# A two-layer mixture of experts on one core: the order of its head, and an eight-byte gather ahead of the first gather

## The chip, the cores and the metric

The kernel runs on one core of a Trainium2 chip. The metric is device time in microseconds (us) of one execution, and times are given as medians over runs. A profiled execution gives the span from the first to the last instruction; the execution's own time lies a little above it.

## The reference, cut to what matters

Three layers follow each other on 7168 tokens of 192 numbers: a causal convolution whose seven weights per token and head come from a softmax, and two mixtures of experts with eight experts each (two experts a token in the first, one in the second).

```python
def _attn_ref(x, weight_gen):
    w = weight_gen - np.max(weight_gen, axis=-1, keepdims=True)
    w = np.exp(w)
    w = w / (np.sum(w, axis=-1, keepdims=True) + 1e-09)
...
    out = np.einsum('bshk,bskhg->bshg', w, x_unf)

def _moe_ref(x, w_gate, w_noise, noise, w1, w2):
    logits = x @ w_gate
    noise_scale = np.log1p(np.exp(x @ w_noise))
    noisy_logits = logits + noise_scale * noise
    top2 = np.argpartition(-noisy_logits, 2, axis=1)[:, :2]
...
            h = np.maximum(x[mask] @ w1[e], 0.0)
            out[mask] += top2_w[mask, k, None] * (h @ w2[e])

def _moe2_ref(x, w_gate, w1, w2):
    expert_idx = np.argmax(logits, axis=1)
...
        h = np.maximum(xe @ w1[e], 0.0)
        ye = h @ w2[e]
        out[mask] = gate_w[mask, None] * ye
```

## The kernel before

The kernel writes all engines' instructions in one program, and a small scheduler decides their order while the program is built. Each piece of work is a generator (a thread of `Feed`, line 212) that yields the engine and the tiles it will need next. A `Clock` (line 78) keeps an estimate of when each engine and tile is free; `Feed.until` and `Feed.pump` always let the thread with the smallest estimated start go on, plus a bias in microseconds that was given when the thread was added (a negative bias favours it). Nothing of this runs on the chip: what is left is a fixed order on each engine's queue, and each queue is strictly in order. Nearly all instructions are recorded through one helper, so they carry line 190 in the profile and are told apart by their tiles.

The tokens of the first routed phase are 2 half batches of 12 token columns; the convolution treats them as six items of four columns: items 0 to 2 of the first half batch, 3 to 5 of the second. For an item VectorE multiplies tokens by softened weights, two taps at a time (`TAPS`, three steps of 1536 numbers a partition and one of 768, tile `prod`, three buffers: `PB`), and TensorE sums them with products by the identity (tile `acc`, two products of 128x384 a tap, each of which the profile counts as two records; 28 records an item). Then `split_rows` (622) scales the sum and splits it into two halves of fp16 (tiles `sx`, `rows`), the rows go to memory, are transposed (`xtg`), and `logit_thread` (707) multiplies them by the gate's weights (`gwh`, `gwl`, result `pm`, then `lg`).

Before that, `first_loads` (755) brings tokens and convolution weights, `first_soft` (794) softens the weights in four pieces (tile `wmxa`, a piece of 4 and one of 8 columns for each half batch; the weights themselves lie in `wres`), and `prep_gate` (428) loads the gate's weights (`gwr`), squares them on ScalarE (sum `gwa`), sums that over partitions with one product of the ones matrix on TensorE (into `pm`) and scales them on VectorE (`gwt`, `gwh`, `gwl`). `weight_lane` (469) does the same with the experts' weights in pieces W1 and W2 of 0.79 MB, two lanes of two buffers (`w`, sum `wacc`, product into `pm`, scale `wsc`); the first pieces are loaded by GpSimd's queue once a copy (`spacer`) has seen the first half batch's last tokens. After item 5, `choose` and `route_` (1048) pick the experts and compute the indices of the blocks (`sli`: block numbers, `src`: rows to gather), TensorE does 64 products without use (`NFILL`), and the experts begin: GpSimd gathers 128 rows at a time (`gt`), TensorE transposes the first ones (`ph` from `gt`), multiplies by W1 and W2 and so on to the end of the program.

Of the kernel before, what the change touches and what calls it, by code (L numbers as in the profile page):

```python
# [8 lines left out]
F32 = mybir.dt.float32  # L9
# [7 lines left out]
P = 128  # L17
D = 192
E = 8
# [10 lines left out]
W1FIRST = 0  # L30
CLATE = 20.0
W2LATE = -0.1
WLATE = 0.0
W1LATE = 0.0
PLATE = -2.0
VPE = -100.0
# [18 lines left out]
HT = 2  # L55
TP = 1
LT = 0.0
NFILL = 64
TB = 2
AB = 1  # L60
OBG = 0
# [211 lines left out]
def moe_kernel(ctx: ExitStack, tc: tile.TileContext, x: bass.AP, wgen: bass.AP,  # L273
               g1: bass.AP, n1: bass.AP, noise: bass.AP, w11: bass.AP, w12: bass.AP,
               g2: bass.AP, w21: bass.AP, w22: bass.AP, out: bass.AP):
    nc = tc.nc
# [3 lines left out]
    feed = Feed(clk)  # L280
    nc.scalar.preload_act_table_set("natural_log_exp_and_others")

    def new_pool(name, side=None, **kw):
        if side:
            kw["side"] = side
        return Pool(tc.alloc_tile_pool(name=name, bufs=1, **kw), clk, name.startswith("ps"))
# [19 lines left out]
    def small_ps():  # L306

        while ps_lock:
            yield None
        ps_lock.append(1)  # L310
        return psum.tile([P, 512], F32, name="pm")
# [12 lines left out]
    for pi, (m, g, ja, jb, full) in enumerate(((0, 0, 0, JS, True), (0, 0, JS, JA, False), (0, 1, JA, J, False),  # L324
                                               (1, 0, 0, JA, True), (1, 1, JA, J, False))):
        ph = Ph()
# [42 lines left out]
    raw = new_pool("raw", side="right")  # L369
# [55 lines left out]
    gw = [None, None]  # L425
    ngs = [2 * E, E]

    def prep_gate(m):
        srcs = [g1, n1] if m == 0 else [g2]
        n = E * len(srcs)  # L430
        a = raw.tile([P, 2, n], F32, name=f"gwr{m}")
        for i, s in enumerate(srcs):
            SP.dma_start(a[:, 0, i * E:(i + 1) * E], s[0:P])
            SP.dma_start(a[0:64, 1, i * E:(i + 1) * E], s[P:D])
            SP.dma_start(a[64:P, 1, i * E:(i + 1) * E], s[P:D])
        h = const.tile([P, 2, n], F16, name=f"gwh{m}")
        acc = const.tile([P, 1], F32, name=f"gwa{m}")
        yield "A", a
        A.activation(h, a, AF.Square, accum_out=acc)
        yield "P", acc  # L440
        ps = yield from small_ps()
        yield "P", acc, ps
        PE.matmul(ps[:, 0:1], onesf, acc, start=True, stop=True)
        t = const.tile([P, 4], F32, name=f"gwt{m}")
        yield "V", ps[:, 0:1]
        pow2(ps[:, 0:1], t[:, 0:1], t[:, 1:2], t[:, 2:3], 10)
        ps_lock.clear()
        lo = const.tile([P, n], F16, name=f"gwl{m}")
        V.tensor_scalar(h, a, t[:, 1:2], None, op0=ALU.mult)
        V.scalar_tensor_tensor(lo, a[:, 0], t[:, 1:2], h[:, 0], op0=ALU.mult, op1=ALU.subtract)  # L450
        V.scalar_tensor_tensor(h[64:P, 1], a[64:P, 1], t[64:P, 1:2], h[64:P, 1],
                               op0=ALU.mult, op1=ALU.subtract)
        gw[m] = (h, lo, t[:, 2:3])
# [301 lines left out]
    def first_loads():  # L755
        h = K - 1
        for b in range(B):
            G.memset(x0[b][0:1, 0:h], 0.0)
        def weights(b, a, z):
            SP.dma_start(g0[b][:, a * H:z * H].rearrange("p a k -> p (a k)"), bass.AP(  # L760
                tensor=wgen.tensor, offset=wgen.offset + (b * S + a) * H * K,
                ap=[[J * H * K, P], [1, (z - a) * H * K]]))

        def tokens(b, a, z):
            SP.dma_start(x0[b][:, h + a:h + z].rearrange("p j d -> p (j d)"), xrows(b, 0, P, a, z - a))

        for b in range(B):
            yield "S", x0[b]
            weights(b, 0, NJ)
            tokens(b, 0, NJ)  # L770
            for p0, np_ in ((16, P - 16), (1, 15)):
                SP.dma_start(x0[b][p0:p0 + np_, 0:h].rearrange("p j d -> p (j d)"), xrows(b, p0, np_, -h, h))
            tokens(b, NJ, 2 * NJ)
            weights(b, NJ, JS)
            tokens(b, 2 * NJ, JS)
            if b == 0:

                G.tensor_copy(spacer, x0[0][0:1, h + JS - 1, 0:1])
            loaded.append(b)
# [14 lines left out]
    def first_soft():  # L794
        for b in range(B):
            for a, z in ((0, NJ), (NJ, JS)):
                mx = raw.tile([P, JS * H], F32, name="wmxa")[:, 0:(z - a) * H]
                yield from soften(g0[b][:, a * H:z * H], mx, z - a)
                soft0[b].update(range(a, z))
                yield ()  # L800

    def conv_lane(items, early, pool, ln):
# [40 lines left out]
        while cur:  # L843
            r, i = cur
            lane_th[ln][2] = 0.0 if phases[1].ready else CLATE if r.g else BLATE if r.j0 and not started else 0.0
            b, ja, n = subs_of(r)[i]
# [29 lines left out]
            if on_pe:  # L876
                acc = psp.tile([P, 2, 512], F32, name=f"acc{ln}")
                k = 0
                for m in TAPS:
                    t = raw.tile([P, max(TAPS), NJ * D], F32, name="prod", bufs=PB)[:, 0:m, 0:n * D]  # L880
                    yield "V", t
                    taps(t, k, m)
                    yield "P", t, acc
                    for i in range(m):
                        for a in range(0, n, 2):
                            PE.matmul(acc[:, a // 2, 0:2 * D], identf, t[:, i, a * D:(a + 2) * D],
                                      start=(k + i == 0), stop=(k + i == K - 1))
                    k += m
                acc = acc[:, 0:n // 2, 0:2 * D].rearrange("p a (b d) -> p a b d", b=2)
                t = t[:, 0].rearrange("p (a b d) -> p a b d", b=2, d=D)  # L890
            else:
                acc = pool.tile([P, NJ, D], F32, name=f"acc{ln}", bufs=1 if ln else AB)[:, 0:n]
                prod(acc, 0)
                last = None
                for k in range(1, K):
                    yield "V",
                    t = pool.tile([P, NJ, D], F32, name="tmp", bufs=TB)[:, 0:n]
                    prod(t, k)
                    if k == K - 1 and q and XB == 1 and not ln:
                        nxt = yield from load(*q)  # L900
                    if last is not None:
                        V.tensor_tensor(acc, acc, last, op=ALU.add)
                    last = t
                yield "V",
                V.tensor_tensor(acc, acc, last, op=ALU.add)
# [142 lines left out]
    def route_(r):  # L1048
        ph, nt = r.ph, r.nt
# [145 lines left out]
        sf, si = [rt.tile([P, 2 * NTM], dt, name=v)[:, 0:nc2 * nt] for v, dt in (("slf", F32), ("sli", I32))]  # L1195
# [42 lines left out]
        for k, (reg, c0, n) in enumerate(groups):  # L1238
# [11 lines left out]
            for v in range(n):  # L1250
                PE.matmul(tp[:, reg * nb:(reg + 1) * nb], oh[:, :, v], ob[:, :, v],
                          start=(lo + v == 0), stop=(lo + v == 15 or c0 + v == nw - 1))
        if r is rts[0]:
            idle = psp.tile([P, 2, 512], F32, name="acc0")
            for _ in range(NFILL):
                nc.tensor.matmul(idle[:, 0, 0:P], ident, ident, start=True, stop=True)
# [156 lines left out]

    queue, lqueue, turned, pending, routing = [], [], [], [False] * 4, []
    todo = {"load": 0, "turn": 0}
    lane_th, w_th = [], []
    pools = []

    def hurry():
# [23 lines left out]
    gps = {(0, g): new_group(0, g) for g in range(2)}  # L1443
    rts = [new_route(ph, gps[0, ph.g]) for ph in phases[:3]]
    feed.add(first_loads(), -9.0)
    feed.add(first_soft(), -1.0)
    logit_ths = [feed.add(turn_thread(), LLATE), feed.add(logit_thread(), LLATE)]
    items = [(r, i) for r in rts for i in range(r.n)]
    early = [(r, i) for r, i in items if r is rts[0] or r is rts[1] and i < BPE]
# [3 lines left out]
    pieces = [(e, k) for e0 in range(0, E, WG) for k in range(2) for e in range(e0, e0 + WG)]  # L1453
    for k in range(2):
        w_th.append(feed.add(weight_lane(0, f"w{k}", pieces, k), WLATE))
    feed.add(prep_gate(0))
    feed.add(prep_gate(1))

    def noises():
        for r in rts:  # L1460
# [294 lines left out]
    for i in range(nu + 1):  # L1755
# [30 lines left out]
        n = max(n1, n2)  # L1786
# [66 lines left out]
```

## Time and profile before

| what | value |
|---|---|
| median of 3 runs (lowest to highest) | 982.63 us (980.37 to 986.98) |
| the profiled execution, its own time | 985.76 us |
| its span | 983.9 us |
| mean granted TensorE clock | 0.964 of 2.4 GHz |
| TensorE busy | 901.3 us (92%) |
| VectorE, ScalarE, GpSimd busy | 754.2, 514.0, 429.7 us |
| last convolution sum of the first phase ends | 88.64 us |
| first product of the experts begins | 129.63 us |

The profile is of one execution. A row of a timeline gives a start, a length and the instruction; in brackets stands how long its engine had been idle and what ended that. PE is TensorE, PEld its weight loads, DVE VectorE, ACT ScalarE, POOL GpSimd, SP the engine that issues most DMAs. The clock column is the clock granted to TensorE as a share of 2.4 GHz; 0.50 is 1.2 GHz.

### The profile page before, as it was taken

The page shows a single profiled execution, that of the slowest core. Times are in us where ns is not written, and L with a number is a line of the kernel's source. Part 1 is how long each engine was busy: PE and PEld are TensorE (multiplying, and loading weights), DVE is VectorE, ACT ScalarE, POOL GpSimd, SP SyncE. Part 2 cuts the span into 40 slices and gives each one's busy share as a digit, 9 for nine tenths or more (in the row PEclk, how much of TensorE's full clock was granted, in tenths as well). Part 3 has the DMA queues.
Part 4 walks back from the last instruction along what each step waited for, and adds up shares of the span by engine and source line. Part 5 has one row for each costly group of instructions (what it writes and reads, how often), then busy time and mean ns, then how long its engine had stood idle before and what let it go on. Part 6 is the DMA issues. An engine that isn't in the chain of part 4 may idle for free. (4 is left out here: it accounts for less than half of the span.)

```text
span 983.9 us, 26950 instructions
## 1 busy us (share of the span) xinstructions
PE 901.3 (92%) x10522; PEld 834.1 (85%) x10522; DVE 754.2 (77%) x1827; ACT 514.0 (52%) x1040; POOL 429.7 (44%) x574
## 2 busy tenths in 40 slices
PE   1897388899999999999999998999989999999996
PEld 0554388899998999999999998989989999999986
DVE  8587887889998999978498787798588886355453
ACT  1334068674533454653487797645766533444332
POOL 4020044565544555543454453343554544564552
PEclk8898599999999999999999999999999999999998
DMA  9256059968542895852478999853677447462692
GB/s 283 70 136 145 1 152 266 253 156 193 149 116 64 182 215 99 232 131 75 108 200 195 264 264 230 200 121 100 168 173 172 114 123 225 88 118 80 200 258 85
DMA packets 206161, 157.56 MB, mean 160 GB/s; under 512 B 134412, under 2 KB 184927, under 8 KB 206028
## 3 DMA queue, kind: packets, MB, share of 16 engines
q1 hardware_dynamic: 187292, 110.93, 46.2%
q0 software_dynamic: 18736, 44.85, 17.9%
q8 instruction: 84, 1.38, 0.6%
q14 instruction: 49, 0.40, 0.2%
HBM read 74.46 MB, written 32.59 MB: 109 GB/s over the span
## 5 line engine op out<-in xcount | busy, mean ns | idle before, releaser
L190 ACT ACTIVATE hh<-ph 128x512 f16<-128x512 f32 x362 | 214.8, 595 | 261.9 <-PE ph L190 254.8
L190 DVE SCALAR_TENSOR_TENSOR hl<-ph,hh 128x512 f16<-128x512 f32 x362 | 245.6, 684 | 108.7 <-ACT hh L190 100.5
L190 PE MATMUL ph<-xt,wres 128*128 128x256 f16 (+1 forms) x3200 | 320.9, 252 | 4.4 <-ACT xt L190 1.4
L190 PEld LDWEIGHTS <-wres 128*128 128x128 f16 x3200 | 261.5, 99 | 24.4 <-issue 3.9
L190 PE MATMUL py<-wres,hh 128*128 128x192 f16 x2048 | 273.1, 247 | 1.0 <-ACT yo L190 0.8
L190 PEld LDWEIGHTS <-hh 128*128 128x128 f16 x2896 | 260.6, 98 | 5.8 <-issue 1.7
L190 POOL DMA_INDIRECT gt<-rows,src x181 | 197.4, 1091 | 139.4 <-issue 119.7
L190 PE MATMUL py<-wres,hl 128*128 128x192 f16 x1024 | 252.5, 247 | 0.0
L190 POOL DMA_INDIRECT ybuf<-yo,dest x120 | 134.0, 1116 | 250.6 <-ACT yo L190 234.0
L190 PEld LDWEIGHTS <-hl 128*128 128x128 f16 x1448 | 141.9, 98 | 0.5 <-DVE hl L190 0.4
L190 PE MATMUL ph<-xt,w 128*128 128x128 f16 (+1 forms) x1600 | 135.4, 238 | 3.7 <-DMA w<-wres 2.0
L190 PEld LDWEIGHTS <-w 128*128 128x128 f16 x1600 | 113.9, 98 | 10.4 <-DVE w L190 2.6
L190 PE MATMUL py<-w,hh 128*128 128x192 f16 x848 | 113.2, 246 | 0.0
L190 POOL DMA_INDIRECT out_dram<-yo,dest x61 | 62.1, 1018 | 113.9 <-ACT yo L190 71.7
L190 PE MATMUL py<-w,hl 128*128 128x192 f16 x424 | 104.3, 246 | 0.2 <-DVE hl L190 0.2
L190 PE MATMUL acc<-prod,identf 128*128 128x384 f32 x168 | 62.1, 528 | 13.1 <-DVE prod L190 10.7
L190 PEld LDWEIGHTS acc<-prod,identf 128*128 128x128 f32 x168 | 33.8, 206 | 35.4 <-DVE prod L190 10.7
L190 DVE COPY w<-wres 128x3072 f16 x53 | 51.2, 967 | 8.2 <-issue 5.2
L190 DVE SCALAR_TENSOR_TENSOR wres<-w,wsc,wres 128x1024 f16<-128x1024 f32 (+1 forms) x32 | 49.6, 1550 | 7.6 <-ACT wres L190 6.9
L190 ACT ACTIVATE yo<-py 128x192 f32<-128x192 f32 x120 | 37.8, 328 | 28.2 <-PE py L190 22.8
L190 ACT ACTIVATE wres<-w,wsc 128x1024 f16<-128x1024 f32 (+1 forms) x32 | 43.5, 1361 | 10.1 <-DVE wsc L190 9.3
L190 ACT ACTIVATE wres<-w 128x1536 f16<-128x1536 f32 x32 | 47.3, 1477 | 1.6 <-DMA w<-in_moe_w_dram 1.6
(216 smaller groups left out, 930.3 us busy)
## 6 DMA issues: line engine op xcount, KB each, us to landing
w<-wres SPq DMA_DIRECT2D x46, 384.0 KB
rows<-rows SPq DMA_DIRECT2D x24, 512.0 KB
w<-in_moe_w_dram SPq DMA_DIRECT2D x14, 768.0 KB
w<-in_moe_w_dram SPq DMA_DIRECT2D x13, 512.0 KB
xs<-in_x_dram SPq DMA_DIRECT2D x6, 960.0 KB
rows<-ybuf SPq DMA_DIRECT2D x10, 384.0 KB
yl<-ybuf SPq DMA_DIRECT2D x10, 384.0 KB
wres<-wbt SPq DMA_DIRECT2D x56, 64.0 KB
```

The costliest lines, as they stand in the source:

```text
L190: return fn(*args, **kw)
```

## The change

Softening gets another bias after its first piece (0.3 in place of -1.0). The loads of the first layer's gate weights move into `first_loads`, ahead of the last tokens of the first half batch. `prep_gate` gets a bias of -2 and squares gate 0 only when one item's products have been written, gate 1 when two have. When the block numbers of the first phase are known, GpSimd gathers 128 rows of 8 bytes into a tile that is no longer used, and 56 products without use take the place of 64.

```diff
-NFILL = 64
+SLATE = 0.3
+GLATE = -2
+GP = 1
+NFILL = 56
...
+    gwr = {}
+
+    def load_gate(m):
         srcs = [g1, n1] if m == 0 else [g2]
-        n = E * len(srcs)
-        a = raw.tile([P, 2, n], F32, name=f"gwr{m}")
+        a = gwr[m] = raw.tile([P, 2, ngs[m]], F32, name=f"gwr{m}")
         for i, s in enumerate(srcs):
...
+    def prep_gate(m):
+        n = ngs[m]
+        if m:
+            load_gate(m)
+        while m not in gwr:
+            yield None
+        a = gwr[m]
         h = const.tile([P, 2, n], F16, name=f"gwh{m}")
         acc = const.tile([P, 1], F32, name=f"gwa{m}")
+        while len(summed) <= m * GP:
+            yield None
         yield "A", a
...
             weights(b, NJ, JS)
+            if b == 0:
+                load_gate(0)
             tokens(b, 2 * NJ, JS)
...
                 soft0[b].update(range(a, z))
+                soft_th[2] = SLATE
                 yield ()
...
                     k += m
+                summed.append(1)
...
         if r is rts[0]:
+            nc.gpsimd.indirect_dma_start(out=sf[:, 0:2], out_offset=None, in_=ph.rows[0:ph.upto * P, 0:256].rearrange("n (a b) -> (n a) b", b=2),
+                                         in_offset=bass.IndirectOffsetOnAxis(ap=si[:, 0:1], axis=0))
             idle = psp.tile([P, 2, 512], F32, name="acc0")
...
-    lane_th, w_th = [], []
+    lane_th, w_th, summed = [], [], []
...
-    feed.add(first_soft(), -1.0)
+    soft_th = feed.add(first_soft(), -1.0)
...
-    feed.add(prep_gate(0))
-    feed.add(prep_gate(1))
+    feed.add(prep_gate(0), GLATE)
+    feed.add(prep_gate(1), GLATE)
```

On TensorE, at the start of the program, this is the order before (`acc0` and `acc1` are the two lanes' sums, so acc0_184 is item 0 and acc1_240 item 1; the product into pm_231 is the first gate's):

```order
L190 MATMUL acc0_184<-prod_185,identf_78 128x384 x4
L190 MATMUL pm_231<-gwa0_169,onesf_86 128x1
L190 MATMUL acc0_184<-prod_193,identf_78 128x384 x4
L190 MATMUL acc1_240<-prod_241,identf_78 128x384 x4
L190 MATMUL acc0_184<-prod_247,identf_78 128x384 x4
L190 MATMUL acc1_240<-prod_253,identf_78 128x384 x4
L190 MATMUL acc0_184<-prod_269,identf_78 128x384 x2
L190 MATMUL acc1_240<-prod_275,identf_78 128x384 x4
L190 MATMUL pm_263<-gwa1_175,onesf_86 128x1
```

and this is the order now, with acc1_227 as item 1 and acc0_279 as item 2:

```order
L193 MATMUL acc0_184<-prod_185,identf_78 128x384 x4
L193 MATMUL acc0_184<-prod_191,identf_78 128x384 x4
L193 MATMUL acc0_184<-prod_203,identf_78 128x384 x4
L193 MATMUL acc0_184<-prod_217,identf_78 128x384 x2
L193 MATMUL pm_233<-gwa0_166,onesf_86 128x1
L193 MATMUL acc1_227<-prod_228,identf_78 128x384 x4
L193 MATMUL acc1_227<-prod_250,identf_78 128x384 x4
L193 MATMUL pm_270<-wacc0_219,onesf_86 128x1
L193 MATMUL acc1_227<-prod_265,identf_78 128x384 x4
```

All of item 0 now stands ahead of the gate's product, which stood behind its first four; the first expert weight's product (pm_270) stands inside item 1.

On VectorE, at the same place, before (the first row is the last of the softening of both half batches; gwt0, gwh0 and gwl0 are the first gate's scaling):

```order
L190 TENSOR_TENSOR wres_112<-wres_112,wmxa_211 128x448
L190 TENSOR_TENSOR prod_193<-wres_112 128x1536
L190 TENSOR_TENSOR prod_241<-wres_112 128x1536
L190 TENSOR_TENSOR prod_247<-wres_112 128x1536
L190 TENSOR_TENSOR prod_253<-wres_112 128x1536
L190 TENSOR_SCALAR gwt0_233<-pm_231 128x1
L190 TENSOR_SCALAR gwt0_233<-gwt0_233 128x1 x3
L190 TENSOR_SCALAR gwh0_168<-gwr0_161,gwt0_233 128x32
L190 SCALAR_TENSOR_TENSOR gwl0_259<-gwr0_161,gwt0_233,gwh0_168 128x16
```

and now, from the first product step on:

```order
L193 TENSOR_TENSOR prod_185<-wres_112 128x1536
L193 TENSOR_TENSOR prod_191<-wres_112 128x1536
L193 TENSOR_REDUCE wmxa_183<-wres_112 128x64
L193 TENSOR_TENSOR wres_112<-wres_112,wmxa_183 128x448
L193 TENSOR_TENSOR prod_203<-wres_112 128x1536
L193 TENSOR_REDUCE wmxa_183<-wres_112 128x64
L193 TENSOR_SCALAR wmxa_183<-wmxa_183 128x64
L193 RECIPROCAL wmxa_183<-wmxa_183 128x64
L193 TENSOR_TENSOR wres_112<-wres_112,wmxa_183 128x448
L193 TENSOR_TENSOR prod_217<-wres_112 128x768
L193 TENSOR_TENSOR prod_228<-wres_112 128x1536
```

Product steps now stand between the pieces of the first half batch's softening, and the softening of the second half batch follows later, at item 2.

On VectorE again, behind the last sum, before (xtg are the copies of the last transposes, lg the logits):

```order
L190 TENSOR_SCALAR lg_127<-pm,ix_126,gwt_233 128x64
L190 SCALAR_TENSOR_TENSOR rows_624<-acc_506,sx_125,rows_624 128x4x192
L190 TENSOR_REDUCE ex<-ra 128x16
L190 TENSOR_TENSOR oh_129<-ie,ex 128x128
L190 CAST xtg<-acc_661 128x512
L190 CAST xtg<-acc_673 128x512
L190 TENSOR_SCALAR lg_127<-pm,ix_126,gwt_233 128x64
```

and now, where wsc_660 and exp_104 belong to the second expert's W2:

```order
L193 SCALAR_TENSOR_TENSOR rows_632<-acc_537,sx_125,rows_632 128x4x192
L193 TENSOR_REDUCE ex<-ra 128x16
L193 TENSOR_TENSOR oh_129<-ie,ex 128x128
L193 CAST xtg<-acc_649 128x512
L193 TENSOR_SCALAR wsc_660<-pm 128x1
L193 TENSOR_SCALAR exp_104<-wsc_660 128x1
L193 TENSOR_SCALAR wsc_660<-exp_104 128x1
L193 TENSOR_SCALAR lg_127<-pm,ix_126,gwt_235 128x64
L193 CAST xtg<-acc_686 128x512
L193 TENSOR_SCALAR lg_127<-pm,ix_126,gwt_235 128x64
```

The scale of a weight piece and one step of logits now stand between the two copies.

On GpSimd the only new instruction is the small gather, right ahead of the first gather of rows.

## Rows read from the trace of the kernel before

**Rows 1.** The page, busy time by engine: us, share, instructions.
```profile
PE 901.3 (92%) x10522; PEld 834.1 (85%) x10522; DVE 754.2 (77%) x1827; ACT 514.0 (52%) x1040; POOL 429.7 (44%) x574
```

**Rows 2.** Windows: length; busy us of PE, PEld, DVE, ACT, POOL; clock; DMA.
```profile
14.00:25.00 11.00, 0.00 (x0) 0.00 (x0) 9.63 (x14) 1.01 (x3) 1.78 (x3) 0.60 1.07 315
...
25.00:30.00 5.00, 4.67 (x9) 2.85 (x10) 0.00 (x1) 2.84 (x7) 0.00 (x0) 0.50 0.41 103
...
60.00:89.00 29.00, 29.00 (x161) 17.60 (x160) 23.82 (x37) 9.65 (x18) 0.00 (x0) 1.00 0.78 175
...
89.00:130.00 41.00, 17.74 (x165) 14.95 (x162) 33.15 (x111) 4.57 (x11) 3.20 (x3) 0.58 0.06 18
```

**Rows 3.** Timeline, head: start, us, engine, line, instruction, [idle before <-releaser].
```profile
9.36 4.58 PE L190 MATMUL acc<-prod,identf 128*128 128x384 f32 x8 [9.36 <-DVE prod L190]
...
19.92 5.09 DVE L190 TENSOR_TENSOR prod<-wres 128x1536 f32<-128x1536 f32 x3
...
24.96 0.23 ACT L190 ACTIVATE gwh<-gwr 128x32 f16<-128x32 f32 x1 [7.09 <-DMA gwr<-in_moe_w_noise_dram]
...
25.33 0.59 PE L190 MATMUL pm<-gwa,onesf 128*128 128x1 f32 x2 [11.39 <-ACT gwh L190]
...
30.71 1.76 DVE L190 TENSOR_TENSOR prod<-wres 128x1536 f32<-128x1536 f32 x1 [5.71 <-PE acc L190]
```

**Rows 4.** Timeline, weight loads of the products' records from 29.76 us.
```profile
29.76 11.90 PEld L190 LDWEIGHTS acc<-prod,identf 128*128 128x128 f32 x37 [0.30 <-issue]
```

**Rows 5.** Timeline, single VectorE steps of the head.
```profile
17.90 0.62 DVE L190 TENSOR_REDUCE wmxa<-wres 128x64 f32<-128x448 f32 x1 [0.64 <-ACT wres L190]
...
32.57 0.40 DVE L190 TENSOR_SCALAR gwt<-gwt 128x1 int32<-128x1 int32 x3
...
40.68 0.53 DVE L190 TENSOR_SCALAR sx<-sx 128x1 f32<-128x1 f32 x3 [1.27 <-ACT prod L190]
...
48.20 1.28 DVE L190 SCALAR_TENSOR_TENSOR wres<-w,wsc,wres 128x1024 f16<-128x1024 f32 x1
...
51.07 0.74 DVE L190 SCALAR_TENSOR_TENSOR wbt<-w,wsc,wbt 128x512 f16<-128x512 f32 x1
...
54.16 0.34 DVE L190 TENSOR_SCALAR lg<-pm,ix,gwt 128x64 f32<-128x64 f32 x1 [1.04 <-PE pm L190]
...
56.79 1.01 DVE L190 SCALAR_TENSOR_TENSOR rows<-acc,sx,rows 128x768 f16<-128x768 f32 x1
...
69.23 0.15 DVE L190 TENSOR_SCALAR wsc<-pm 128x1 f32<-128x1 f32 x1
```

**Rows 6.** Timeline, items 3 to 5 on TensorE, first and last stretch.
```profile
59.52 11.88 PE L190 MATMUL acc<-prod,identf 128*128 128x384 f32 x36 [1.30 <-DVE prod L190]
...
84.52 4.12 PE L190 MATMUL acc<-prod,identf 128*128 128x384 f32 x12
```

**Rows 7.** Timeline, from the indices to the first expert's product.
```profile
124.97 0.20 DVE L190 CUSTOM_DVE_ANT_0 src<-rb,rc 128x80 uint16<-128x80 uint16 x1
...
126.19 1.59 POOL L190 DMA_INDIRECT gt<-rows,src  x1 [67.48 <-issue]
...
128.09 0.97 POOL L190 DMA_INDIRECT gt<-rows,src  x1 [0.30 <-issue]
...
129.63 0.38 PE L190 MATMUL ph<-ident,gt 128*128 128x128 f16 x4 [1.65 <-issue]
```

**Rows 8.** TensorE's waits 129 to 260 (us, times, longest), and two of them.
```profile
PE pm L190 <- ACT wres L190: 4.0, 3, 2.5
...
165.04 0.38 PE L190 MATMUL pm<-wacc,onesf 128*128 128x1 f32 x2 [0.23 <-ACT wres L190]
...
181.04 0.38 PE L190 MATMUL pm<-wacc,onesf 128*128 128x1 f32 x2 [2.47 <-ACT wres L190]
```

**Rows 9.** DMA queues, 14 to 18 and 18 to 20 us: packets, MB, share.
```profile
q0 software_dynamic: 244, 0.83, 66.3%
...
q1 hardware_dynamic: 123, 0.00, 5.5%
```

More of the change, by code (lines that the diff above doesn't have):

```diff
@@ L32 @@
 W2LATE = -0.1
-WLATE = 0.0
+WLATE = 0
 W1LATE = 0.0
@@ L426, in moe_kernel @@
     ngs = [2 * E, E]
-    def prep_gate(m):
+    gwr = {}
+    def load_gate(m):
         srcs = [g1, n1] if m == 0 else [g2]
-        n = E * len(srcs)
-        a = raw.tile([P, 2, n], F32, name=f"gwr{m}")
+        a = gwr[m] = raw.tile([P, 2, ngs[m]], F32, name=f"gwr{m}")
         for i, s in enumerate(srcs):
```

## The prediction

> **What bounds the kernel now.** I read the share of busy time first: TensorE is busy for 92% of the span [rows 1], so time is to be had only where it stands. The windows of the head come next. From 14 to 25 us TensorE does nothing, and from 89 to 130 us it is busy for 17.74 us of 41; between 60 and 89 us it is never idle [rows 2]. So the head has two different limits, and the change touches both. The timeline says what the first hole is: the first eight product records begin at 9.36, then TensorE waits 11.39 us for the squared gate weights, whose square on ScalarE (24.96) had waited for the load of the noise half [rows 3]. Behind that one in-order product the convolution's sums stand still; VectorE fills its three product buffers and then waits 5.71 us for TensorE as well [rows 3]. Nothing in the hole is work. A later hole is the same in kind: among the experts' products TensorE waits three times, 4.0 us in all, for a squared weight piece [rows 8].
>
> **The convolution's sums.** The change takes the gate's product out from behind the first four products and puts it behind item 0 (an item is four token columns of one half batch, six items in all), and lets softening of the second half batch wait. What is late next is found by following the two queues with the durations of before.
> TensorE again starts at 9.36. Eight records took 4.58 us there [rows 3], against 11.90 us for 37 of them later, 0.32 each [rows 4]: the early ones ran at half pace, whatever the clock column says ahead of its first change; from 25 to 30 us, at a granted 0.50 (1.2 GHz), the same half pace is seen after 11 us without work, and full pace (2.4 GHz) from 29.76 on, 4.4 us after the restart [rows 2 to 4]. So item 0's first eight records end at 13.9 and its other twenty need 20 x 0.32 = 6.4 us: 20.4. VectorE keeps up: three more product steps and the softening of the rest of the first half batch lie before 17. I add 0.5 us in case the clock rises later than it did: 20.9. The gate's product then goes at once, as its load of 32-byte rows has ten microseconds to land; VectorE, which has one product step in stock, waits for it and scales the gate (seven small steps, the middle three 0.40 together [rows 5]: 1.5 us with their gaps): it is free at about 22.9.
> From there VectorE is the limit. Ahead of item 3's first product its new order holds: five full product steps at 5.09 / 3 = 1.70 [rows 3] and two half ones (0.9, estimated as half), 10.3; two scales (0.53 and one more step of 0.15) and row steps (1.01), 3.4; three weight scales at some 0.57 (three steps of 0.15 and gaps), 1.7; two W1 pieces at 1.28 + 0.74, 4.0; the softening of the second half batch, five passes of 0.62 for its larger part and about two thirds of that for the smaller, 5.3; the second gate, 1.5; one step of logits, 0.34 [rows 5]. Sum 26.5: item 3's first product begins at 49.4 and ends at 51.1. Before, TensorE began item 3 at 59.52 and ended item 5 at 84.52 + 4.12 = 88.64, 29.1 us without a gap [rows 2, 6]. The changed kernel has the same products and three groups of logits there. But now TensorE stands nearly still from about 42 to 51, since softening and weights come in one block on VectorE; it will restart at half pace, and 4.4 us at half pace lose 2.2. End of the sums: 51.1 + 2.2 + 29.1 = 82.4 against 88.64, **a gain of 6.2 us**, not the 11.4 of the wait: softening is put off, not removed, and it stands in TensorE's way later. Bounds: 9 if the clock stays up and nothing waits, 3 if the first W1 piece lands late (below) and the clock takes longest.
>
> **The tail up to the routing.** Between the last sum and the first gather the steps are the same in number, but one weight piece's scale (0.57 on VectorE) and the logits of item 4 (0.34) now stand between the last two transposes instead of ahead of them, while the last row step comes 0.3 sooner: **0.7 us lost**, with 0 and 1.5 as bounds. The fill products (56 for 64) end before the first gather has landed in either case; I cost them at nothing, and at full pace eight of them are 0.4 us if that cover is gone.
>
> **The small gather.** It stands on GpSimd's queue behind weight loads that are long done and waits for the block numbers, some 13 us ahead of the first real gather; behind it on that queue is only that gather, so the wait holds nobody. No row of before shows a gather of 8 bytes; its own price is hidden in those 13 us. What it may give: the first gather began 1.02 us after its indices were written and took 1.59, the second 0.30 after the one before and took 0.97, and TensorE's first product on it started at 129.63 after 1.65 us of idling [rows 7]. If all of the excess belongs to a first use, 0.72 + 0.62 = 1.34 come back one for one; if none, nothing. I take the 0.62 and some of the start, **0.9 us**, since the duration is the nearer comparison and the first gather has more waits to pass than the second.
> The stretch from the indices (125.17) to the product is 4.46 us in all [rows 7]. The Trainium skill, GPSIMD Engine Reference, section 2.1 Instruction dispatch, gives about 6 us for the first call of freshly loaded code, in no visible instruction; so much does not fit into 4.46, and the sum by it would end at the third rival's.
>
> **The experts' first stretch.** The order of weight pieces changes: the second expert's W2 is squared and scaled in the head instead of among the first experts' products, and a second W1 piece (experts 2 and 3) is loaded there. After the start ten pieces have to stream instead of eleven, and the last one's product stands about 9 us of TensorE work earlier though most stand later than their number before. The three waits of 4.0 us [rows 8] should shrink; the pieces landed some 5 us apart (165.04 and 181.04 are the products of the fourth and the seventh [rows 8]), so one piece less helps each of them. **I take 2.2 us**, with 4 and -1 as bounds, since the fifth piece now stands no later than before.
>
> **Sum.** 6.2 - 0.7 + 0.9 + 2.2 = 8.6 us. The profiled execution took 985.76 with a span of 983.9, so it would take 977.2; it lies 3.1 above the median of the three runs, 982.63, and the forecast against that is **974.0**. Later stages have the same products, and their start only moves.
>
> **Rivals.**
> A, all ends well: TensorE keeps its pace through the softening block, the experts' waits vanish, the gather gives all. 8.4 - 0.4 + 1.3 + 4 = 13.3, 969.3. For it: each part is within its bound; against: TensorE lost its pace in under 11 us of idling before.
> B, the wait moves: TensorE runs in order, and now a product on a weight piece takes the gate's place, in the head or among the experts, whose other vector work also comes earlier. Half the head's gain and none of the experts': 3.1 - 0.7 + 0.9 = 3.3, 979.3. For it: this is just what the gate's product did.
> C, the first use of a gather costs the landing too: of the 4.46 us only the second gather's 0.30 + 0.97 would stay, 3.2 instead of 0.9 come back, 971.7.
> D, slower: the six gate loads are put ahead of the first half batch's last token load, and the copy that releases the W1 loads waits for this. Between 18 and 20 us the hardware queue, which then held the gate loads, moved 123 packets and no whole 0.01 MB while the weight pieces streamed on the software queue [rows 9]: small packets crawl, until the square could start at 24.96 [rows 3]. If they crawl ahead of the token load too, some 9 us go on top of the first W1 piece (0.79 MB), which by the bytes of its queue had landed at about 18 [rows 9]. It has until 22.9 before ScalarE's row step waits behind its square, so D decides from a delay of 5 us and loses one for one; at 9 us plus a second piece behind it, some 11.6 us are lost, and 8.6 turns into -3: 985.6. Against it: at that place no software queue is running.
> The Trainium skill, DMA: Bandwidth & Descriptors, section SWDGE vs HWDGE vs iDMA, says that an engine takes the software and hardware queues in turn; by that rule D does not happen, and the trace agrees as far as the crawl is seen only while both run.
> That the change does not do what it says would be B.
>
> **How the numbers follow.** Forecast 0.57, A 0.13, B 0.17, C 0.07, D 0.06. One per cent is 9.8 us, about what a measurement of this kernel can tell from no change; 8.6 is inside it. The forecast's own bounds (its terms' errors together some 4 us) are 970 to 978, with a third of its chance beyond one per cent: 0.20; with A and C, faster is 0.40. B, the rest of the forecast and half of D stay within: 0.57. Slower keeps the other half of D: 0.03. The range takes in A's upper part and B: 968 to 980.5.
>
> **What will show it.** The 11.39 us wait should be gone and item 0 be one run of 28 records; item 3 should begin near 51 behind an idle stretch of 6 to 9 us with a granted 0.50; the last sum should end near 82.5, the first gather take about 1.0 us, and the first expert product come near 123. I am wrong if item 3 begins after 55, if a product on a weight piece waits over 3 us, or if the experts' stretch takes longer than before.

## The result, and the profile after

The changed kernel takes **969.54 us** (median of four runs, 968.54 to 971.06) against 983.21 for the kernel before on the same chip (median of four runs, 980.37 to 986.98): ratio 0.9863, 95% interval 0.9826 to 0.9899, 13.7 us or 1.4% faster. The forecast was 974.0 in a range of 968.0 to 980.5: the sign was right and the time inside the range, but 8.6 us had been forecast and 13.7 came. By the two profiled executions it is 985.76 to 969.38, 16.4 us; the one of before lay 2.5 over its median, so sums over the two traces come out some 2.5 us larger than the gain of the medians.

The page's row of TensorE answers to [rows 1]; the share rises by one point while the work is the same.

```profile
PE 895.8 (93%) x10514; PEld 830.0 (86%) x10514; DVE 754.8 (78%) x1827; ACT 513.1 (53%) x1040; POOL 440.3 (46%) x578
```

Windows of after (columns as in [rows 2]): the old hole, the new one, the tail with the routing, and the first 5 us of the experts (for a later section).

```profile
14.00:25.00 11.00, 10.29 (x34) 5.96 (x33) 8.91 (x20) 2.65 (x5) 4.16 (x7) 1.00 1.05 329
42.00:51.00 9.00, 1.92 (x5) 1.13 (x5) 8.65 (x23) 6.64 (x12) 3.30 (x7) 0.80 0.90 259
...
89.00:130.00 41.00, 19.82 (x193) 17.68 (x191) 33.01 (x103) 5.69 (x11) 9.04 (x8) 0.59 0.10 21
123.99:128.99 5.00, 4.27 (x47) 4.14 (x48) 4.56 (x10) 2.17 (x4) 3.78 (x5) 0.68 0.37 108
```

The hole of 14 to 25 us is filled. A smaller one has opened at 42 to 51, where VectorE is busy for 8.65 of 9 us: the softening that was put off stands there in one block. From 89 to 130 us TensorE works as little as before (19.82 us of 41, before 17.74): the routing has only moved.

The head and the tail on the timeline of after; they answer to [rows 3, 6].

```profile
10.07 10.82 PE L193 MATMUL acc<-prod,identf 128*128 128x384 f32 x28 [10.07 <-DVE prod L193]
20.73 0.28 PE L193 MATMUL pm<-gwa,onesf 128*128 128x1 f32 x2
...
49.73 10.18 PE L193 MATMUL acc<-prod,identf 128*128 128x384 f32 x24 [5.72 <-DVE sx L193]
76.91 4.12 PE L193 MATMUL acc<-prod,identf 128*128 128x384 f32 x12
80.86 0.28 PE L193 MATMUL pm<-wacc,onesf 128*128 128x1 f32 x2
87.91 0.15 DVE L193 TENSOR_SCALAR wsc<-pm 128x1 f32<-128x1 f32 x1
88.11 0.17 PE L193 MATMUL pm<-gwh,xtg 128*128 128x16 f16 x1 [1.48 <-DVE wsc L193]
88.65 1.01 PE L193 MATMUL acc<-ident,rows 128*128 128x128 f16 x8
91.42 0.34 DVE L193 TENSOR_SCALAR lg<-pm,ix,gwt 128x64 f32<-128x64 f32 x1 [0.40 <-PE pm L193]
```

Item 0 is one run of 28 records, and the gate's product (20.73) waits for nothing. Item 3 begins at 49.73 behind 5.72 us of idling, and 24 records take 10.18 us, 0.42 each where 0.32 is full pace. The last sum ends at 81.03 (88.64 before). Then something is new: at 88.11 the logits of item 4 wait 1.48 us for the first step of the scale of a weight piece (87.91), whose product (80.86) was put ahead of them, and eight transposes stand behind that. The last logits end at 91.76, 10.7 us after the last sum; before, that step took 8.8, since its last logits stood at 97.10:

```profile
97.10 0.34 DVE L190 TENSOR_SCALAR lg<-pm,ix,gwt 128x64 f32<-128x64 f32 x1 [0.40 <-PE pm L190]
```

From the small gather to the first expert product, timeline of after, against [rows 7]:

```profile
106.49 1.44 POOL L1272 DMA_INDIRECT slf<-rows,sli  x1 [60.09 <-DVE blkh L193]
119.35 0.20 DVE L193 CUSTOM_DVE_ANT_0 src<-rb,rc 128x80 uint16<-128x80 uint16 x1
119.47 1.81 DVE L193 SCALAR_TENSOR_TENSOR wres<-w,wsc,wres 128x1536 f16<-128x1536 f32 x1
120.49 1.64 POOL L193 DMA_INDIRECT gt<-rows,src  x1 [12.57 <-issue]
...
123.99 0.38 PE L193 MATMUL ph<-ident,gt 128*128 128x128 f16 x4 [2.52 <-issue]
```

A gather has now run on this queue 13 us earlier, and the first real one still takes 1.64 us (1.59 before); indices to product is 4.44 us against 4.46.

TensorE's waits in the first 131 us of the experts, the view of [rows 8]:

```profile
PE pm L193 <- ACT wres L193: 0.3, 1, 0.3
```

Waits for squared weight pieces fell from 4.0 to 0.3 us. By the two traces, the time from the first expert product to the second products on the second group's gathered rows fell from 188.72 to 181.26 us, and the rest of the span from 665.55 to 662.35. Timeline of before, then of after:

```profile
318.35 1.06 PE L190 MATMUL ph<-ident,gt 128*128 128x128 f16 x8
```

```profile
305.25 0.61 PE L193 MATMUL ph<-ident,gt 128*128 128x128 f16 x8
```

### The profile page after: what moved, and what is told of

Read it like the earlier page. It is cut to its first block, busy times and chain, and to the rows that moved or that the text cites. A ratio compares the mean times of both kernels' runs of the same rounds, so it can differ in the third digit from the quotient of the medians.

```text
span 967.6 us, 26940 instructions
## 1 busy us (share of the span) xinstructions
PE 895.8 (93%) x10514; PEld 830.0 (86%) x10514; DVE 754.8 (78%) x1827; ACT 513.1 (53%) x1040; POOL 440.3 (46%) x578
## 3 DMA queue, kind: packets, MB, share of 16 engines
q0 software_dynamic: 19008, 45.64, 19.1%
## 4 chain that ended last, share of the span: by engine, by line
PE 36%; DVE 7%; DMA 2%; ACT 2%; issue 2%; SPq 1%; DVEq 0%; POOL 0%; POOLq 0%; ACTq 0%
PE ph L193 18%; PE py L193 15%; PE pm L193 2%; DVE hl L193 2%; DMA yl<-ybuf 1%; SPq L193 1%; ACT hh L193 1%; DVE w L193 1%; DVE yl L193 1%; ACT rows L193 1%; PE pr L193 1%; DMA w<-wres 1%; DVE rows L193 0%; DVE tab L193 0%; DVE xtg L193 0%
## 5 line engine op out<-in xcount | busy, mean ns | idle before, releaser
L193 POOL DMA_INDIRECT ybuf<-yo,dest x120 | 138.1, 1151 | 232.7 <-ACT yo L193 217.6
L193 POOL DMA_INDIRECT gt<-rows,src x181 | 200.4, 1107 | 82.9 <-issue 62.4
```

The lines of the kernel that those rows point to most:

```text
L193: return fn(*args, **kw)
```

## The experiments

The experiments ran on three other chips, on which the kernel before takes 1039 to 1049 us (last section). So whole times are given as ratios to the kernel before on the same chip, and single steps are read in the traces: from the last logits to the indices every trace but one (named below) has 27.7 to 27.8 us, as the first chip has. The controls share a chip with the runs on the weight piece behind the logits and on VectorE's scale; the other ratios are of the two other chips, and comparing them with the controls' assumes that the ratio holds from chip to chip.

**Controls.** Kernel before and changed kernel, unchanged, on one of those chips.

> The kernel before, unchanged, for a second trace. In the first one 16.4 us lie between the two profiled executions: 5.6 up to the first expert product, 4.5 in the next 120 us, and some 6 later, where before had two dips of the granted clock (at 316 and 610 us) behind waits of 1.1 us and more. Theory: the head's 5.6 and the waits for weight pieces come back in any execution, the two later dips belong to one execution or one chip; so this trace shows the 11.4 us wait and waits for weight pieces of 3 to 5 us, and dips at other places. Rival: the later dips are fixed by the order and stand at the same products again.

> The changed kernel, unchanged, as the control of the next two and of the four that ran on a chip on which the kernel before takes 1049 us. Expected ratio to before 0.986 within 0.004 on either sort of chip. Rival: on a slower chip, where the experts wait more for transfers, the ratio is nearer to 1 (0.990 to 0.995), since only the head's part is left.

The ratio is 0.987 (0.9824 to 0.9917): the gain is there on a slower chip too, as forecast, though the interval still takes in the lower end of the rival's 0.990 to 0.995. The trace of before again: last sum 89.56, first expert product 130.58; of after again: 80.88 and 123.70. The sums give 8.7 and the tail takes 1.95 back. From the first expert product to the second group's product it is 197.04 against 192.16 us, then 704.88 against 701.34. Waits for weight pieces are 3.1 against 1.9 us here. Of the later dips of the granted clock in before, the one at 316 us comes back at its place in the work (at 321), so there the rival was right; the one at 610 does not. Timeline of the first chip's before, then of before again, where the second group's rows are gathered:

```profile
310.87 0.98 POOL L190 DMA_INDIRECT gt<-rows,src  x1 [0.30 <-DVE m L190]
315.37 0.40 PE L190 MATMUL ph<-ident,gt 128*128 128x128 f16 x4 [1.11 <-DMA gt<-rows,src]
316.45 2.10 PE L190 MATMUL ph<-xt,wres 128*128 128x256 f16 x10 [0.69 <-ACT xt L190]
```

```profile
314.84 0.98 POOL L190 DMA_INDIRECT gt<-rows,src  x1 [0.30 <-issue]
319.44 0.40 PE L190 MATMUL ph<-ident,gt 128*128 128x128 f16 x4 [1.22 <-DMA gt<-rows,src]
322.19 0.33 ACT L190 ACTIVATE yo<-py 128x192 f32<-128x192 f32 x1 [3.77 <-remote]
325.53 2.29 PE L190 MATMUL ph<-xt,wres 128*128 128x256 f16 x10 [5.69 <-ACT xt L190]
```

In after the same gather starts 7.9 us ahead of its product, and nothing waits:

```profile
290.79 0.98 POOL L193 DMA_INDIRECT gt<-rows,src  x1 [0.30 <-DVE be L193]
298.64 0.61 PE L193 MATMUL ph<-ident,gt 128*128 128x128 f16 x8
```

**One half of the change at a time.** First the softening's rule put into the kernel before (with the small gather and 56 fill products), the gate as before:

```diff
+SLATE = 0.3
...
                 soft0[b].update(range(a, z))
+                soft_th[2] = SLATE
```

> The kernel before with the softening's rule, the small gather and 56 fill products of the changed one, but the gate loaded and squared as before. Theory: what costs 11.4 us before is a product placed ahead of its operand; here the order puts the gate's product behind 18 products of the sums by itself, where TensorE arrives near 23 to 25 us, so at most some 3 us of that wait are left and the time is within 4 us of the changed kernel: 970 to 974. Rival: the early gate load is what removes the wait, and without it the gate's square stays at 25 and everything behind it too: 977 to 983.

Then the gate's half, the softening as urgent as before:

```diff
-SLATE = 0.3
+SLATE = -1.0
```

> The changed kernel with the softening as urgent as before (all four pieces are softened ahead of nearly all products), the gate loaded early and squared late as in the changed one. Theory: the wait moves. The order now puts the first weight piece's product behind 8 products, and that piece lands near 23 us, so TensorE waits there some 8 to 11 us with the same consequences as the gate before: 978 to 985. Rival: gate alone carries the gain, softening order is worth little: 969 to 973.

Softening alone: ratio 1.0013 (0.9981 to 1.0044); last sum at 94.20, later than before by 4.6. My theory fell. Its trace shows why it had looked at the wrong queue:

```profile
25.66 0.23 ACT L191 ACTIVATE gwh<-gwr 128x32 f16<-128x32 f32 x1 [12.60 <-DMA gwr<-in_moe_w_noise_dram]
26.03 0.38 PE L191 MATMUL pm<-gwa,onesf 128*128 128x1 f32 x2 [2.36 <-ACT gwh L191]
29.11 0.53 DVE L191 TENSOR_SCALAR sx<-sx 128x1 f32<-128x1 f32 x3 [7.52 <-ACT prod L191]
...
52.30 12.00 SPq L191 DMA_TRANSPOSE xtg<-rows  x2
59.51 0.20 PE L191 MATMUL pm<-gwh,xtg 128*128 128x16 f16 x1 [3.27 <-DMA xtg<-rows]
```

TensorE's own wait for the gate is down to 2.36 us, as I had said. But the square waits 12.60 us on ScalarE's in-order queue, item 0's row step stands behind it there, and VectorE waits 7.52 us for that; a pair of transposes of the rows then takes 12.00 us (pairs take up to 9.50 in the other traces), and logits wait for them.

Gate alone: ratio 0.9964 (0.9938 to 0.999), last sum at 92.64. The wait moved, as the theory said, though not to the piece that it named, whose product waits 1.66 us and not 8 to 11: TensorE waits three times, 9.0 us in all, for weight pieces whose products now stand ahead of sums, the longest time for 6.13.

```profile
48.42 0.59 PE L193 MATMUL pm<-wacc,onesf 128*128 128x1 f32 x2 [6.13 <-ACT wres L193]
```

Neither half brings the sums' end forward; both together bring it forward by 7.6.

**The gate loads at their old place**, all else as changed:

```diff
-        if m:
-            load_gate(m)
+        load_gate(m)
...
-            if b == 0:
-                load_gate(0)
```

> The changed kernel with the gate's loads at their old place, behind the token loads; the gate is still squared behind item 0. The order has the same head up to the fourth item, but more weight pieces in it and fewer behind. Theory: the small packets crawl while the weights stream, so the square comes at 25 as before; TensorE waits some 4 us for it behind item 0, VectorE waits for the gate's product (3 to 5 us), and the sums end at 83 to 87 instead of 81; the experts may give back 1 to 4 for the pieces done early. Ratio 0.986 to 0.992. Rival: six early loads cost the first weight piece what they save the gate; then the sums end at 80 to 81.5 here too, the first products come 0.7 us sooner, and the ratio is under 0.986.

Ratio 1.0023 (0.9996 to 1.0049): the whole gain is gone. The last sum ends at 98.57, far later than either theory said.

```profile
24.31 0.58 PE L193 MATMUL pm<-gwa,onesf 128*128 128x1 f32 x2 [3.92 <-ACT gwh L193]
24.93 0.16 DVE L193 TENSOR_SCALAR gwt<-pm 128x1 f32<-128x1 f32 x1 [6.62 <-PE pm L193]
52.90 0.58 PE L193 MATMUL pm<-wacc,onesf 128*128 128x1 f32 x2 [5.03 <-ACT wres L193]
```

The 3.92 is as expected, the 6.62 more than the 3 to 5 expected; the rest is not the gate. More weight pieces stand in this head, TensorE waits 5.03 us for one, and VectorE is busy for 67.23 us between first product and last sum, against 61.68 in the changed kernel. So of the 17.7 us by which the sums end later than in the control, the wait of 3.92 is the early loads' in place; the rest stands in another order that the planner then makes, and this run does not show how it divides. Rival D's price is small: the first product began at 9.02 to 9.88 us in the four traces with late loads, and at 9.19 to 10.73 in those with early ones.

**VectorE's work ahead of item 3.**

```diff
-WLATE = 0
+WLATE = 1.5
```

> The changed kernel with the weight pieces' steps put behind the sums by a bias of 1.5, the experts' order as changed. Theory (the prediction's walk): VectorE's work ahead of item 3's first product sets the end of the sums. Without two W1 pieces (4.0 us) and three weight scales (1.7) there, item 3 begins at 43 to 45 instead of 49.7 and the last sum ends at 74 to 77 instead of 81; but the pieces come later, the first expert products wait for them, and I expect a loss of 2 to 8 us there: ratio 0.985 to 0.995. Rival: TensorE, not VectorE, sets the end of the sums; it stays at 79 to 82 and the ratio is over 0.99.

Item 3 begins at 45.62, a little behind the forecast, and the last sum ends at 75.57, 5.3 earlier than in the control: VectorE's walk does set the end of the sums. But the ratio is 0.9979 (0.9947 to 1.001), for a larger loss behind the sums than I had expected. The pieces' steps land in the tail (16.6 us instead of 10.7, one wait of 5.00 for a transposing DMA) and in the routing (31.9 instead of 27.7; the named exception), and the experts take 205.9 us from their first product to the second group's (333.57 less 127.72) instead of 192.2. What the prediction's walk gains for the sums is paid back behind them more than once.

```profile
45.62 22.91 PE L193 MATMUL acc<-prod,identf 128*128 128x384 f32 x64 [1.90 <-DVE prod L193]
84.41 0.19 PE L193 MATMUL pm<-gwh,xtg 128*128 128x16 f16 x1 [5.00 <-DMA xtg<-rows]
```

**The small gather left out**, and **64 fill products** for 56, on one chip:

```diff
-            nc.gpsimd.indirect_dma_start(out=sf[:, 0:2], out_offset=None, in_=ph.rows[0:ph.upto * P, 0:256].rearrange("n (a b) -> (n a) b", b=2),
-                                         in_offset=bass.IndirectOffsetOnAxis(ap=si[:, 0:1], axis=0))
```

```diff
-NFILL = 56
+NFILL = 64
```

> The changed kernel without the 8-byte gather, all else the same. Theory now (against my prediction's +0.9 for the small gather): the first real gather takes 1.6 us with or without it, because VectorE's 1.81 us scale of a weight piece with two operands in SBUF, which stands right behind the indices, is in progress when the gather begins (0.70 of 1.59 us before, 0.80 of 1.64 us after), and not because of a first use. So: time as the changed kernel, 969.5 within 0.5; first gather 1.5 to 1.7 us; indices to first expert product 4.4 us. Rival, first use, as predicted: about 0.9 us slower (0.6 to 1.3), 970.4, and a first gather longer than 1.64 or later after its indices than 0.94.

> The changed kernel with 64 fill products again in place of 56. Theory: the eight fewer leave TensorE idle for 2.5 us ahead of the first expert product instead of 1.65, and the granted clock falls to one half from 125.8 to 129.2, which the first ten thousand columns of the experts show as 1.4 us lost against before; with 64 the clock stays at 1.0 there and 1.4 us (0.7 to 1.7) come back: 968.1. Rival (the prediction's): the fill is covered in either case, 969.5 within 0.4.

Ratios 0.9889 (0.9864 to 0.9914) and 0.985 (0.9821 to 0.988), too near to part by time. The trace without the small gather: first gather 1.62 us, beginning 1.01 after its indices instead of 0.93, first expert product 4.54 instead of 4.44 after them. So by this trace the small gather is worth 0.1 us. With 64 fill products TensorE idles 1.74 us ahead of the first product, and the granted clock stays at 1.00 in the first 5 us of the experts, where the changed kernel had 0.68 on the first chip and 0.71 as control. But 56 also kept 1.00 in five of ten traces, the one without the gather among them (idle 2.32), so the number of fill products alone does not decide it; three of these five fell to 0.50 some 7 to 9 us behind the first product, at further idling of 2.2 to 4.0 us. The theory is not shown, only that none of four traces with 64 lost the clock there.

**VectorE's scale moved away from the first gather.**

```diff
                     yield "V", d[:, :, 0:D]
+                    while filled and not phases[0].placed:
+                        yield None
+                        yield "V", d[:, :, 0:D]
                     V.scalar_tensor_tensor(d[:, :, D:2 * D], w, sc, d[:, :, 0:D], op0=ALU.mult, op1=ALU.subtract)
...
             idle = psp.tile([P, 2, 512], F32, name="acc0")
+            filled.append(1)
```

> The changed kernel, with the 1.81 us scale of the second expert's W2 moved on VectorE from right behind the indices to behind the routing's small steps. Theory: a gather that begins while VectorE works on two operands in SBUF lasts 0.83 us plus what is left of that step (0.80 of 1.64 here); without it the first gather takes 0.95 to 1.0 us and the first expert product comes 0.6 to 0.7 us sooner after its indices (3.75 to 3.9 instead of 4.43). Rival, the first gather is slow for its own sake: it still takes 1.5 to 1.65 us. The whole gains 0.3 to 0.7 by the theory, which is at the edge of what the rounds can tell, so the trace decides.

```profile
120.17 0.20 DVE L193 CUSTOM_DVE_ANT_0 src<-rb,rc 128x80 uint16<-128x80 uint16 x1
121.30 0.96 POOL L193 DMA_INDIRECT gt<-rows,src  x1 [12.54 <-issue]
123.32 1.81 DVE L193 SCALAR_TENSOR_TENSOR wres<-w,wsc,wres 128x1536 f16<-128x1536 f32 x1
123.82 2.12 POOL L193 DMA_INDIRECT gt<-rows,src  x1 [0.30 <-issue]
124.11 0.38 PE L193 MATMUL ph<-ident,gt 128*128 128x128 f16 x4 [1.57 <-issue]
```

The first gather takes 0.96 and its product comes 3.74 us after the indices instead of 4.4: the theory holds, and the gather that the scale now meets (123.82) takes 2.12. Ratio 0.985 (0.98 to 0.9899), not told from the control's 0.987.

**The weight piece behind the logits.**

```diff
+            while m == 0 and k and ln and not started and rts[0].done < rts[0].n:
+                yield None
             yield "P", acc
```

> The changed kernel, with the second expert's W2 product (the fourth weight piece) held until the head's last rows are out, so that the two groups of logits and the transposes pass ahead of it. Theory: the tail lost 1.9 us instead of the 0.7 of the prediction because item 4's logits and eight transposes stood behind a wait of 1.48 us for that piece's scale; without it the time from the last sum's end to the last logits falls from 10.7 to 8.8 to 9.4 us, and the whole by 1.3 to 1.9 us. Rival: the scale's steps then stand behind the logits on VectorE and the gain is at most 0.5; or nothing is gained since the piece comes later for the experts.

The tail falls from 10.75 to 9.24 us: item 4's logits reach VectorE at 84.22, and thirteen transposes follow in one run.

```profile
84.22 0.34 DVE L193 TENSOR_SCALAR lg<-pm,ix,gwt 128x64 f32<-128x64 f32 x1
85.98 1.57 PE L193 MATMUL acc<-ident,rows 128*128 128x128 f16 x13 [0.16 <-ACT rows L193]
...
89.75 0.34 DVE L193 TENSOR_SCALAR lg<-pm,ix,gwt 128x64 f32<-128x64 f32 x1 [0.40 <-PE pm L193]
```

The place is as the theory says; the whole (0.9855, 0.9809 to 0.99; median 1025.22 against the control's 1025.16) does not show it.

**All three mends** (the piece, the scale, 64 fill products):

> The changed kernel with the fourth weight piece's product behind the logits, its scale behind the routing's small steps, and 64 fill products. Theory: the three gains add, as they lie one behind the other: tail 9.2 instead of 10.75, indices to first expert product 3.75 instead of 4.4, so the first expert product near 121.5 to 122 and the ratio 0.002 to 0.003 under that of the changed kernel (0.983 to 0.985). Rival: what is gained in the head is lost among the experts, since the held piece comes later there: first expert product as said, ratio 0.986 to 0.988.

The first expert product comes at 120.78, 2.9 earlier than in the control (tail 9.26, indices to product 3.73); the ratio is 0.9875 (0.9848 to 0.9902). That is the rival's number, but its interval and the control's cover each other, so whether the 2.9 us of the head are kept stays open (2.1 of them are the tail and the gather, the rest lies ahead of the last sum, which the mends do not touch). It is not shown to beat the changed kernel.

**The second group's routing held back.**

```diff
+        due = clk.free["P"] + 6
+        while r is rts[1] and clk.free["P"] < due:
+            yield None
         yield from route(r)
```

> The changed kernel, with the second group's routing held back by 6 us of planned TensorE time and nothing else, so that its last step and the first products on its gathered rows stand where they stood before (157 and 163 us of TensorE work behind the first expert product, against 149 and 158). Theory: a part of the gain that the prediction did not see comes from here. Before, these gathers start 3 us ahead of the first product on them; TensorE waits 1.1 to 1.2 us for the landing, then 0.7 to 5.7 us for ScalarE's copy, and its clock falls. So 4 to 8 us are lost against the changed kernel (ratio 0.991 to 0.996), with these two waits in the trace near 170 to 190 us behind the first expert product. Rival: the later gains belong to the weight pieces, which stay as changed; ratio 0.985 to 0.988 and no such wait.

The ratio is 0.993 (0.9901 to 0.9959), in the theory's range: by the middle values about half of the gain, though the interval meets the control's, of another chip, at 0.990 to 0.992; on this chip the three mends had 0.9875. The trace is less clear. It is of the slowest of the twelve executions (1040.6 us, median 1033.02), and the gather starts 10.7 us ahead of its product, because ScalarE stands still for 7.93 us there for nothing that the profile names, so the expected wait of 1.1 us has no room to show.

```profile
318.71 0.98 POOL L193 DMA_INDIRECT gt<-rows,src  x1 [0.30 <-issue]
327.80 0.60 ACT L193 ACTIVATE hh<-ph 128x512 f16<-128x512 f32 x1 [7.93 <-remote]
329.42 1.06 PE L193 MATMUL ph<-ident,gt 128*128 128x128 f16 x8
```

Before again idles at the same point of the work (3.77, above); the changed kernel's control has 0.96 there. So the times speak for a price of several us for the place in the order, but neither of the two waits is shown to be it: on the first chip they are 1.11 and 0.69, with a slow 2.10 behind them, and on these chips the idling that nothing explains covers them.

## Why the prediction came out right, and where it was too small

**The convolution's sums: 6.2 forecast, 7.6 measured** (8.7 on the second chip). The walk held: gate's product at once, item 3 behind a block of softening, restart at half pace. From item 3's start to the last sum's end the trace has 31.30 us, the forecast 29.1 + 2.2. The difference is VectorE's sum up to there, 26.5 us forecast and 25.3 by the trace (22.60 to 47.92), with 0.3 more from the gate's scale, done at 22.6 instead of 22.9: item 3 began at 49.73 instead of 51.1. That VectorE sets this is shown by the run with the weights behind the sums. The argument needed one more condition than it gave: that nothing else waits behind the gate's square on its in-order queue. With late loads and the softening's rule alone item 0's row step did, on ScalarE's (12.60 us).

**The tail: 0.7 lost forecast, 1.9 measured**, over its bound of 1.5. The step costed the moved piece as its VectorE work (0.57) and overlooked that a product of logits waits for its scale and that transposes queue behind that product; holding the piece back returns 1.5. This is rival B's mechanism, in a place that it did not name.

**The small gather: 0.9 forecast, 0.1 measured.** The step that failed is the sentence that the duration is "the nearer comparison" for a first use. The 0.62 were VectorE's: the scale with two operands in SBUF was under way in both traces. The Trainium skill, SBUF — State Buffer, section SBUF: two separate sides, says that the port pair shared by VectorE and GpSimd is an exclusive lock, which a VectorE step with two inputs in SBUF takes against a GpSimd operation that reads SBUF when it starts first; the gather reads its row numbers from SBUF, and the traces agree (0.96 with the scale moved, 1.64 with it).

**The fill products: costed at nothing.** TensorE idled 2.52 us ahead of the first expert product instead of 1.65, and the granted clock over the first 5 us of the experts was 0.68 against 1.00 before; the runs do not show that the number of fill products decides this.

The sums, the tail and the small gather make 6.4 forecast, and the first expert product came 5.6 sooner: nearly right, by errors of both signs, which is luck.

**The experts: 2.2 forecast, 7.5 measured up to the second group, and 3.2 behind it** (4.9 and 3.5 on the second chip). Waits for weight pieces returned 3.7 (1.2 on the second chip), inside the bounds. What failed is the sentence "Later stages have the same products, and their start only moves": in the planner's order the second group's routing ends 8 us of TensorE work sooner (149 against 157 behind the first expert product, counting the columns of the products at full pace), and its gathers no longer land after TensorE wants them. In the first chip's traces TensorE's waits in this stretch, the one for the first gather apart, fell from 8.4 to 2.0 us: 3.7 of that are weight pieces, 1.8 the second group's gathers and the copy behind them (1.11 and 0.69). The order was at hand and I read it only up to the last weight piece. The 3.2 and 3.5 behind the second group are not told from scatter: two other runs of the changed head on the second chip (the weight piece behind the logits, the scale moved) take 708.4 and 705.5 us there, before again 704.88. On the first chip the trace of before has a granted clock of 0.83 at 600 to 620 us and after 1.00 at 590 to 610, but no run ties that to the change.

**Rivals.** A gave the right time for other reasons (the clock was lost at item 3 and the gather gave nothing). C did not happen, and D's delay was 2.4 us (the first weight loads begin at 12.87, before at 10.49), under the 5 from which it decides.

## What to carry to other kernels

A product moved in an order is not free where its operands are squared or scaled on another in-order queue: take the move, the early load and what yields to it as one change, and read every queue that holds a step of that chain, not only the one that shows the wait. Where a planner writes the order, read the new order to its end before saying that later stages only shift. And before a slow first instruction is put down to its being the first, look what another engine is doing in just that stretch.

## What the hardware showed that I had not expected

A gather on GpSimd that begins while VectorE is inside a scale of a weight piece, a step with two operands in SBUF, ends some 0.83 us behind that step, while one that meets no step of VectorE takes 0.94 to 0.99. In after, 120.49 + 1.64 = 122.13 is 0.85 us behind the scale's end at 121.28, and here 203.41 is 0.83 behind 202.58:

```profile
200.76 1.82 DVE L193 SCALAR_TENSOR_TENSOR wres<-w,wsc,wres 128x1536 f16<-128x1536 f32 x1 [0.46 <-ACT wres L193]
200.88 2.53 POOL L193 DMA_INDIRECT gt<-rows,src  x1 [0.30 <-issue]
```

In all fourteen traces 139 gathers of rows begin inside such a scale with more than 0.2 us of it left. Of these 123 end 0.82 to 0.90 us behind it; the other 16, all begun within 0.10 us of its start, last 0.96 to 0.98, as this one of after does, 0.07 us into a scale:

```profile
166.72 0.98 POOL L193 DMA_INDIRECT gt<-rows,src  x1 [0.30 <-issue]
```

The three other chips run the same head to within some 2 us and lose their time behind the first expert product (901.9 us there in before again, 854.3 in before), where engines stand still for nothing that the profile names. In before again:

```profile
ACT hh L190 <- remote: 21.7, 9, 4.0
PE ph L190 <- issue: 9.6, 17, 1.7
```

With two more such rows TensorE's waits for "issue" make 19.1 us. On the first chip the same view has no wait for "remote" and 1.7 us of "issue" in all. What holds the engines there stays open.
